# An S4 and gated-FFN training step on one core: the skip products of the last 16 row tiles made earlier and kept in DRAM

## The chip, the cores and the metric

The kernel runs on one core of one Trainium2 chip. The metric is the device time in microseconds (us) of one execution. A run executes the kernel several times; the time of the kernel before is the median of three. A profile is one execution recorded by the hardware profiler, and its times are that execution's own.

Engines are named as the profile names them: PE (TensorE, matmul), DVE (VectorE), ACT (ScalarE), POOL (GpSimd) and SP (SyncE, which here only issues DMA). Each runs its own instructions in order. A DMA that is issued by SP stands in SP's queue until the buffer that it writes is free and the data that it reads is there.

## The reference

A forward pass and all its gradients. With x of 2048 rows and D = 576 columns, and F = 4608:

```
xn  = layernorm(x)
out = x + (S4(xn) + xn * Dskip) + FFN(xn)
S4(xn)  = causal convolution of xn with a kernel K made from A, B, C, log_dt  (by FFT)
FFN(xn) = (relu(xn Wg) * (xn Wu)) Wd
```

The outputs are `out` (out_0), and for a given grad_out g the gradients of x (out_1), of the S4 parameters, of Dskip and of the three FFN weights. The gradient with respect to xn has the term g * Dskip from the same skip path; the gradient of x follows from it through the layernorm. So there are two skip terms: xn * Dskip in out_0, g * Dskip in the gradient.

## The kernel before

**Rows and chunks.** The 2048 rows are 16 row tiles t of 128, in four groups sg of four. F is cut into 12 chunks c of 384 columns. For each chunk, `a_unit` computes one third (ft) of a group's hidden gradients (three groups of five 512-wide matmuls, then L254 to L264 on VectorE); `outdx` multiplies them back to D columns for one row tile, in four quarters: output and gradient, each in two halves of 288 columns. `dw_down`, `dw_gu` and `dw_left` make the weight gradients of the chunk before. Within a chunk, `gen` yields two `outdx` after each of the first two `a_unit` of a group; the four `outdx` of the last group run one after the other at the start of the next chunk.

**Accumulating.** In chunks 0 to 10 the four quarters of a row tile are copied from PSUM to an SBUF tile `osx` of the pool `ffn_o`, which has three buffers, and added to `acc_dram` in DRAM by a DMA that GpSimd issues (L311 for chunk 0, L313 for the rest). An `osx` buffer is free again when that DMA has landed. PSUM has three banks for the FFN (`ps_mm`), three for S4 (`ps_s4`) and two for transposes (`pt`).

**S4.** The S4 part is a generator that runs beside the FFN, paced against it by the estimated microseconds that both yield. Its intermediate data goes through DRAM. It ends in chunk 11.

**The last chunk.** In chunk 11 `outdx` calls `Final` instead of copying. `Final.load(t)` fetches, on SP's queue and in this order, S3, two halves of Ct, xt, xn and g (the tile `f_xg`), and the accumulated row (`f_acc`), and makes both skip terms at once, L1030: `f_base` = `f_xg` * Dskip, 1152 elements a partition, bf16 in and F32 out. All of them are in a pool of three buffers. `begin(t)` loads up to tile t + 2. `terms` puts S4's last step, x and the accumulated row into the same PSUM group as the FFN's matmuls. `take` (L1049) adds a quarter of PSUM to `f_base`: the output's halves go to `f_o` and out to DRAM, the gradient's halves are written back into `f_base` as F32. `end` (L1058 to L1067) sends the gradient through the layernorm with `f_xg` (row sums on ACT and DVE, L1060 and L1061; L1064 to L1066) and stores it. `f_xg` of a tile is read last by L1066, so the loads of the tile three ahead into the same buffer wait for it.

**Order.** A scheduler of the language orders each engine's instructions from the program's order and its own estimates, so an edit can move other instructions too. `Balance` decides for each PSUM copy whether VectorE or ScalarE does it (L62, L68), from a running account of what both were given.

Of the kernel before, what the change touches and what calls it, by code (L numbers as in the profile page):

```python
# [9 lines left out]
BF16 = mybir.dt.bfloat16  # L10
F32 = mybir.dt.float32
# [3 lines left out]
P = 128  # L15
# [23 lines left out]
class Balance:  # L39


    def __init__(self, nc):
        self.nc = nc
        self.d = 0.0
        self.a = 0.0
# [115 lines left out]
class Ffn:  # L161
    def __init__(self, g, ctx, Wd_in, Wf_in, dWg, dWu, dWd):
        self.g = g
        self.Wd_in, self.Wf_in, self.dWg, self.dWu, self.dWd = Wd_in, Wf_in, dWg, dWu, dWd
        tc, nc = g.tc, g.nc
        pool = lambda name, bufs: ctx.enter_context(tc.tile_pool(name=name, bufs=bufs))
        wp = pool("ffn_w", 1)
        self.wd = [wp.tile([P, NK, Fc], BF16, name=f"wd{i}") for i in range(3)]
        self.wf = wp.tile([P, 3, FTC, D], BF16, name="wf")
        self.hN = wp.tile([P, ST, Fc], BF16, name="hN")  # L170
        self.dgN = wp.tile([P, ST, Fc], BF16, name="dgN")
        self.duN = wp.tile([P, ST, Fc], BF16, name="duN")
        g.xtp = pool("ffn_xt", 2)
        self.tp = pool("ffn_t", 2 * FTC - 1)
        self.ep = pool("ffn_e", 2)
        self.op = pool("ffn_o", 3)
        self.rp = pool("ffn_r", 2)
        self.dp = pool("ffn_d", 4)
        self.T = {}
        self.X = {}  # L180
        self.R = {}
        self.dh0 = {}

    def load_wd(self, c, which=(2, 0, 1)):

# [91 lines left out]
    def outdx(self, c, sg, j, last=None, turns=()):  # L277

        g, nc = self.g, self.g.nc
        t = sg * JS + j  # L280
        js = slice(j * P, (j + 1) * P)
        if last is None:
            o = self.op.tile([P, 2, D], BF16, name="osx")
        else:
            last.begin(t)
        src = self.t_steps(turns)
        Ts = [self.T[(c, sg, ft)] for ft in range(FTC)]
        for which in range(2):
            for hf in range(2):
                hs = slice(hf * DH, (hf + 1) * DH)  # L290
                if which == 0:
                    mms = [(Ts[ft][0], self.wf[:, 0, ft, hs]) for ft in range(FTC)]
                else:
                    mms = [(Ts[ft][1], self.wf[:, 1, ft, hs]) for ft in range(FTC)] + [(Ts[ft][2], self.wf[:, 2, ft, hs]) for ft in range(FTC)]
                mms = [(lt[:, js], rh) for lt, rh in mms]
                if last is not None:
                    mms = last.terms(t, which, hf) + mms
                ps = g.psum_mm.tile([P, 512], F32, name="ps_mm")
                for i, (lt, rh) in enumerate(mms):
                    nc.tensor.matmul(ps[:, :DH], lhsT=lt, rhs=rh, start=(i == 0), stop=(i == len(mms) - 1))  # L300
                if last is None:
                    g.bal.copy(o[:, which, hs], ps[:, :DH], DH)
                else:
                    last.take(t, which, hs, ps[:, :DH])
                next(src, None)
            if which == 0:
                yield FTC * 0.245
        if last is not None:
            last.end(t)
        elif c == 0:  # L310
            nc.gpsimd.dma_start(g.acc_dram[:, t, :, :], o[:])  # L311
        else:
            nc.gpsimd.dma_start(g.acc_dram[:, t, :, :], o[:], accum_op=ALU.add)  # L313
        yield FTC * 0.49
# [158 lines left out]
        return self.q.pop(i)  # L473

class S4:
    def __init__(self, g, par_in, log_dt, outs, Dskip):
        self.g, self.par_in, self.log_dt, self.outs, self.Dskip = g, par_in, log_dt, outs, Dskip
        dram = g.dram
        d = lambda name, shape, dt=BF16: dram.tile(shape, dt, name=name)
        self.s1_dram, self.s3_dram = d("s1_dram", [P, ST, 2, P]), d("s3_dram", [P, ST, 2, P])  # L480
        two = lambda name, shape: [d(f"{name}{hf}", shape) for hf in range(2)]
        self.A = {1: two("A_k", [P, ST, 1, 2, DH]), 2: two("A_ug", [P, ST, 2, 2, DH])}
        self.S = two("S_ug", [ST, P, 2, 2, DH])
        self.C = {1: two("C_dk", [P, ST, 1, 2, DH]), 2: two("C_ydu", [P, ST, 2, 2, DH])}
        self.dk_dram = two("dk_dram", [P, 4, DH // SC, 4, SC])
        self.k_dram = two("k_dram", [P, 4, DH // SC, 4, SC])
        self.dt_dram = d("dt_dram", [P, D], F32)
        self.ex_dram = d("ex_dram", [P, D // SX, SX, NE], F32)

    def pool(self, ctx, name, bufs, side="left"):  # L490
        return ctx.enter_context(self.g.tc.tile_pool(name=name, bufs=bufs, side=side, reuse_waits="tile"))
# [510 lines left out]
class Final:  # L1002

    def __init__(self, g, s4, Dskip, ctx):
        self.g, self.s4, self.Dskip, self.ctx = g, s4, Dskip, ctx
        self.parts = {}

    def load(self, t):  # L1010
        g, nc = self.g, self.g.nc
        if t == 0:
            pool = lambda name, bufs: self.ctx.enter_context(g.tc.tile_pool(name=name, bufs=bufs, reuse_waits="tile"))
            self.dsk = pool("fin1", 1).tile([P, D], BF16, name="dsk")
            nc.sync.dma_start(self.dsk[:], self.Dskip.rearrange("(o d) -> o d", o=1).to_broadcast([P, D]))
            self.pool = pool("fin3", 3)
        S3 = self.pool.tile([P, 2, P], BF16, name="S3")
        nc.sync.dma_start(S3[:], self.s4.s3_dram[:, t])
        Ct = self.pool.tile([P, 2, 2, 2, DH], BF16, name="bC2")
        for hf in range(2):  # L1020
            nc.sync.dma_start(Ct[:, hf], self.s4.C[2][hf][:, t])
        xt = self.pool.tile([P, D], BF16, name="xt")
        nc.sync.dma_start(xt[:], g.x_v[:, t, :])
        xg = self.pool.tile([P, 2, D], BF16, name="f_xg")
        nc.sync.dma_start(xg[:, 0, :], g.xn_dram[:, t, :])
        nc.sync.dma_start(xg[:, 1, :], g.g_v[:, t, :])
        acc = self.pool.tile([P, 2, D], BF16, name="f_acc")
        nc.sync.dma_start(acc[:], g.acc_dram[:, t])
        base = self.pool.tile([P, 2, D], F32, name="f_base")
        nc.vector.tensor_tensor(base[:], xg[:], self.dsk[:].unsqueeze(1).to_broadcast([P, 2, D]), op=ALU.mult)  # L1030
        g.bal.add(d=1.2)
        return S3, Ct, xt, xg, acc, base

    def begin(self, t):
        for n in range(t, min(t + 3, ST)):
            if n not in self.parts:
                self.parts[n] = self.load(n)
        self.o = self.pool.tile([P, 2, D], BF16, name="f_o")

    def terms(self, t, i, hf):  # L1040
        S3, Ct, xt, xg, acc, base = self.parts[t]
# [3 lines left out]

    def take(self, t, i, cols, ps):
        base = self.parts[t][5]
        dst = self.o[:, 0, cols] if i == 0 else base[:, 1, cols]
        self.g.nc.vector.tensor_tensor(dst, base[:, i, cols], ps, op=ALU.add)  # L1049
        self.g.bal.add(d=0.37)  # L1050

    def end(self, t):
        g, nc = self.g, self.g.nc
        S3, Ct, xt, xg, acc, base = self.parts[t]
        o = self.o
        inv_d = 1.0 / D
        xn, gt, dx = xg[:, 0, :], xg[:, 1, :], base[:, 1, :]
        nc.sync.dma_start(g.out0_v[:, t, :], o[:, 0, :])  # L1058
        m = self.pool.tile([P, 4], F32, name="f_m")
        nc.scalar.activation(acc[:, 1, :], dx, ACT.Copy, accum_out=m[:, 0:1])  # L1060
        nc.vector.scalar_tensor_tensor(acc[:, 0, :], dx, 1.0, xn, op0=ALU.mult, op1=ALU.mult, accum_out=m[:, 1:2])  # L1061
        nc.vector.tensor_scalar(m[:, 2:3], m[:, 1:2], -inv_d, None, op0=ALU.mult)
        nc.vector.tensor_scalar(m[:, 3:4], m[:, 0:1], -inv_d, g.rinv[:, t:t + 1], op0=ALU.mult, op1=ALU.mult)
        nc.vector.scalar_tensor_tensor(dx, xn, m[:, 2:3], dx, op0=ALU.mult, op1=ALU.add)  # L1064
        nc.scalar.activation(dx, dx, ACT.Identity, scale=g.rinv[:, t:t + 1], bias=m[:, 3:4])
        nc.vector.tensor_tensor(o[:, 1, :], dx, gt, op=ALU.add)  # L1066
        nc.sync.dma_start(g.out1_v[:, t, :], o[:, 1, :])  # L1067
        g.bal.add(d=2.5, a=1.1)

@with_exitstack  # L1070
def kernel(
# [44 lines left out]

    outs = dict(A_re=out_2, A_im=out_3, B_re=out_4, B_im=out_5, C_re=out_6, C_im=out_7, log_dt=out_8)
    ffn = Ffn(g, ctx, Wd_in, Wf_in, out_10, out_11, out_12)
    s4 = S4(g, par_in, A_log_dt, outs, A_Dskip)
    lnctx, fctx = ExitStack(), ExitStack()  # L1120
    ln_pools = [lnctx.enter_context(tc.tile_pool(name=n, bufs=4)) for n in ("ln_sb", "ln_small")]
    ffn.ln_sb = ln_pools[0]
# [6 lines left out]
            lnctx.close()  # L1129
        return r  # L1130

    final = Final(g, s4, A_Dskip, fctx)
    sgen = s4.gen()
    ft = stt = 0.0
    start = None
# [71 lines left out]
```

## Time and profile before

| what | us |
|---|---|
| median of the three runs (lowest, highest) | 1861.03 (1860.21, 1864.52) |
| the profiled execution, its own time | 1864.52 |
| its span in the trace | 1862.4 |
| PE busy | 1753.3 |
| VectorE busy | 1327.2 |
| ScalarE busy | 1164.1 |
| L1030, all 16: busy, and idle time of VectorE just before it | 21.7, 21.0 |
| `acc_dram` DMAs: median time from issue to landing | 5.0 |
| `f_xg` DMAs (two of 144 KB a tile): the same | 3.9, 4.0 |
| `f_acc` DMAs (288 KB a tile): the same | 4.3 |

The first `outdx` of the last kind starts at 1710.9 us and the last one ends at 1822.5 us. Chunks two to nine lie between about 330 and 1540 us. The mean granted clock of TensorE is 0.991.

How to read what the prediction shows. A window line has the stretch, its length, the busy time of each engine with its number of instructions, the clock granted to TensorE as a share of the full one, the mean busy share of the 16 DMA engines and the rate. A line of waits has the waiting engine, line and tile, what ended the wait, the sum in us, how many and the longest. A group's line has line, engine, operation and shapes, then busy time and the mean of one in ns, then the engine's idle time just before. A timeline line has start and length in us, and in brackets how long the engine stood idle before, and what ended that. L numbers are lines of the kernel before.

### The profile page before, as it was taken

To read this page: it belongs to the slowest core of one execution; us is meant where nothing else is said; L and a number is where in the kernel's file an instruction comes from. 1 tells how busy PE (TensorE), PEld (TensorE's weight loads), DVE (VectorE), ACT (ScalarE), POOL (GpSimd) and SP (SyncE) were. 2 spreads that over 40 slices of the span, in tenths; PEclk is the share of its full clock that TensorE was granted. 3 is DMA by queue.
4 is the path that set the end of the run, shared out by engine and by line. 5 is a ranking of instruction groups with operands and counts; after the bars stand their busy time and mean duration, and the time that the engine had idled before them with its cause. 6 is when DMAs were issued, how large, how long until landed. Compare 5 with 4: busy or idle time off the path is not lost.

```text
span 1862.4 us, 42002 instructions
## 1 busy us (share of the span) xinstructions
PE 1753.3 (94%) x16449; PEld 1222.3 (66%) x16449; DVE 1327.2 (71%) x3041; ACT 1164.1 (63%) x2618; POOL 204.7 (11%) x244
## 2 busy tenths in 40 slices
PE   7989999999999999999989999999999998989889
PEld 5665667667667667666656766766766865666666
DVE  7565784677786886786688789688788774743872
ACT  5864863786586587477378568558658745742442
POOL 0200112011012012011102011101102101100000
PEclk9999999999999999999999999999999999999999
DMA  8889989677568558568667756766846858876863
GB/s 293 272 293 324 321 213 267 189 192 226 165 150 226 170 116 208 167 152 222 193 161 173 222 139 148 225 162 140 220 152 114 206 158 241 236 221 185 247 206 102
DMA packets 215929, 373.25 MB, mean 200 GB/s; under 512 B 49202, under 2 KB 128564, under 8 KB 214196
## 3 DMA queue, kind: packets, MB, share of 16 engines
q1 hardware_dynamic: 189764, 304.08, 50.2%
q0 software_dynamic: 24384, 51.92, 18.6%
q10 hardware_dynamic: 1584, 14.60, 2.2%
q8 instruction: 128, 2.10, 0.5%
q14 instruction: 69, 0.57, 0.1%
HBM read 233.08 MB, written 137.43 MB: 199 GB/s over the span
## 4 chain that ended last, share of the span: by engine, by line
PE 52%; DVE 22%; DMA 12%; ACT 8%; issue 5%; SPq 1%; POOL 1%; ACTq 0%; DVEq 0%; POOLq 0%
PE ps_mm L244 13%; PE ps_mm L300 12%; PE ps_mm L354 10%; PE ps_mm L338 6%; DMA acc_dram<-osx 3%; PE pt L273 2%; DVE pr L902 2%; DVE Sm L903 2%; DVE Y L849 2%; DMA f_xg<-in_grad_out_dram 2%; DVE V L848 1%; DVE Y L847 1%; DVE upm L254 1%; DMA ex_dram<-exs 1%; PE ps_mm L372 1%
## 5 line engine op out<-in xcount | busy, mean ns | idle before, releaser
L68 ACT CAST osx<-ps_mm 128x288 bf16<-128x288 f32 x675 | 258.0, 423 | 78.6 <-PE ps_mm L300 63.9
L313 POOL DMA_DIRECT2D acc_dram<-osx x160 | 138.2, 864 | 1061.0 <-ACT osx L68 594.7
L300 PE MATMUL ps_mm<-wf,dgT 128*128 128x288 bf16 x1152 | 205.6, 287 | 16.6 <-ACT osx L68 9.8
L354 PEld LDWEIGHTS <-rows 128*128 128x128 bf16 x1536 | 146.6, 98 | 92.4 <-issue 2.4
L300 PE MATMUL ps_mm<-wf,duT 128*128 128x288 bf16 x1152 | 206.1, 287 | 0.0
L300 PE MATMUL ps_mm<-wf,hT 128*128 128x288 bf16 x1152 | 184.3, 288 | 6.0 <-DVE hT L256 3.5
L244 PE MATMUL ps_mm<-xT,wd_158 128*128 128x512 bf16 x720 | 180.1, 379 | 4.0 <-DVE osx L62 1.9
L244 PE MATMUL ps_mm<-gT,wd_160 128*128 128x512 bf16 x705 | 179.3, 384 | 4.2 <-ACT obw L68 3.9
L244 PE MATMUL ps_mm<-xT,wd_159 128*128 128x512 bf16 x720 | 180.0, 379 | 0.0
L254 DVE SCALAR_TENSOR_TENSOR upm<-rg,ps_mm 128x512 bf16<-128x512 bf16 x144 | 98.3, 683 | 92.8 <-PE ps_mm L244 64.7
L338 PE MATMUL ps_mm<-rows,hN 128*128 128x144 bf16 x2304 | 161.1, 228 | 0.0
L338 PEld LDWEIGHTS <-hN 128*128 128x128 bf16 x2304 | 150.7, 99 | 7.4 <-issue 4.1
L300 PEld LDWEIGHTS <-dgT 128*128 128x128 bf16 x1152 | 110.2, 98 | 54.0 <-issue 27.5
L68 ACT CAST obw<-ps_mm 128x384 bf16<-128x384 f32 x104 | 49.6, 477 | 146.3 <-PE ps_mm L354 95.5
L354 PE MATMUL ps_mm<-duN,rows 128*128 128x384 bf16 x768 | 136.8, 326 | 0.4 <-DVE upm L254 0.4
L354 PE MATMUL ps_mm<-dgN,rows 128*128 128x384 bf16 x768 | 136.4, 326 | 0.6 <-ACT rg L252 0.6
L300 PEld LDWEIGHTS <-duT 128*128 128x128 bf16 x1152 | 112.7, 98 | 29.1 <-issue 0.5
L300 PEld LDWEIGHTS <-hT 128*128 128x128 bf16 x1152 | 108.0, 98 | 34.3 <-DVE hT L256 5.4
L68 ACT CAST dhb<-ps_mm 128x512 bf16<-128x512 f32 x141 | 83.4, 592 | 65.4 <-PE ps_mm L244 63.9
L252 ACT ACTIVATE rg<-ps_mm 128x512 bf16<-128x512 f32 x144 | 86.8, 603 | 58.7 <-PE ps_mm L244 56.1
L903 DVE TENSOR_REDUCE Sm<-pr 128x8 f32<-128x256 f32 x288 | 119.5, 415 | 4.0
L244 PEld LDWEIGHTS <-wd_160 128*128 128x128 bf16 x705 | 64.7, 98 | 67.9 <-issue 12.9
(2881 smaller groups left out, 3601.5 us busy)
## 6 DMA issues: line engine op xcount, KB each, us to landing
acc_dram<-osx POOLq DMA_DIRECT2D x176, 288.0 KB, 5.0
gT<-in_gT_dram SPq DMA_DIRECT2D x48, 640.0 KB, 6.1
xT<-xT_dram SPq DMA_DIRECT2D x44, 640.0 KB, 5.9
rows<-in_gq_dram SPq DMA_DIRECT2D x48, 576.0 KB, 4.5
wf<-in_Wf_dram ACTq DMA_DIRECT2D x11, 1296.0 KB, 8.9
ex_dram<-exs SPq DMA_DIRECT2D x18, 640.0 KB, 6.2
ex<-ex_dram SPq DMA_DIRECT2D x36, 320.0 KB, 3.7
out_dram<-obw SPq DMA_DIRECT2D x96, 96.0 KB, 2.7
```

The costliest lines, as they stand in the source:

```text
L68: self.nc.scalar.copy(out, in_)
L244: nc.tensor.matmul(ps[:], lhsT=w[:, k, fs], rhs=rhs[:, k, :], start=(k == 0), stop=(k == NK - 1))
L252: nc.scalar.activation(rg[:], ps_g[:], ACT.Relu)
L254: nc.vector.scalar_tensor_tensor(upm[:], rg[:], 0.0, ps_u[:], op0=ALU.is_gt, op1=ALU.mult)
L273: nc.tensor.transpose(out=pt[:, j, :], in_=src[:, j * P:(j + 1) * P], identity=g.ident_bf[:])
L300: nc.tensor.matmul(ps[:, :DH], lhsT=lt, rhs=rh, start=(i == 0), stop=(i == len(mms) - 1))
L313: nc.gpsimd.dma_start(g.acc_dram[:, t, :, :], o[:], accum_op=ALU.add)
L338: nc.tensor.matmul(ps[:, ft * 144:(ft + 1) * 144], lhsT=self.hN[:, st, ft * P:(ft + 1) * P], rhs=gq[:, st, :], start=(st == 0), stop=(st = ...
L354: nc.tensor.matmul(ps[:, :Fc], lhsT=xs[:, st, 0:P], rhs=src[:, st, :], start=(st == 0), stop=(st == ST - 1))
L849: v.tensor_tensor(Y[:], Y[:], V[:], op=ALU.add)
L902: nc.vector.tensor_tensor(pr[:], X[:, dx:dx + DG, r0:r0 + 2].rearrange("p d r a -> p d (r a)").unsqueeze(2).to_broadcast(sh), psg[:, 0:DG ...
L903: nc.vector.tensor_reduce(out=Sm[:, vi, s0 + dd:s0 + dd + DG, :], in_=pr[:], op=ALU.add, axis=AX.X)
```

## The change

The products xn * Dskip and g * Dskip are made in chunks two to nine instead of in the last chunk. In chunk c, `outdx` of the row tiles t with t mod 8 = c - 2 (two a chunk, 16 in all) takes one more `osx` buffer and loads xn and g of that tile into it, on SP's queue. The next `outdx` multiplies that buffer by Dskip in place, all bf16, and SP stores it to a new DRAM tensor `base_dram`. In the last chunk `f_base` is loaded from there, as bf16, behind the other loads of the tile; the gradient's halves go to an F32 tile `f_dx` of their own. Dskip is loaded once at the start, by GpSimd, and stays in SBUF.

```diff
@@ Ffn.outdx, after the four quarters
+        if self.skip is not None:
+            sk, n = self.skip
+            nc.vector.tensor_tensor(sk[:], sk[:], g.dsk[:].unsqueeze(1).to_broadcast([P, 2, D]), op=ALU.mult)
+            g.bal.add(d=0.8)
+            nc.sync.dma_start(g.base_dram[:, n], sk[:])
+            self.skip = None
+        if t % 8 == c - 2:
+            sk = self.op.tile([P, 2, D], BF16, name="osx")
+            nc.sync.dma_start(sk[:, 0, :], g.xn_dram[:, t, :])
+            nc.sync.dma_start(sk[:, 1, :], g.g_v[:, t, :])
+            self.skip = sk, t
         if last is not None:
             last.end(t)
@@ Final.load
-            self.dsk = pool("fin1", 1).tile([P, D], BF16, name="dsk")
-            nc.sync.dma_start(self.dsk[:], self.Dskip.rearrange("(o d) -> o d", o=1).to_broadcast([P, D]))
...
-        base = self.pool.tile([P, 2, D], F32, name="f_base")
-        nc.vector.tensor_tensor(base[:], xg[:], self.dsk[:].unsqueeze(1).to_broadcast([P, 2, D]), op=ALU.mult)
-        g.bal.add(d=1.2)
+        base = self.pool.tile([P, 2, D], BF16, name="f_base")
+        nc.sync.dma_start(base[:], g.base_dram[:, t])
@@ Final.begin
+        self.dx = self.pool.tile([P, D], F32, name="f_dx")
@@ Final.take
-        dst = self.o[:, 0, cols] if i == 0 else base[:, 1, cols]
+        dst = self.o[:, 0, cols] if i == 0 else self.dx[:, cols]
@@ Final.end
-        xn, gt, dx = xg[:, 0, :], xg[:, 1, :], base[:, 1, :]
+        xn, gt, dx = xg[:, 0, :], xg[:, 1, :], self.dx[:]
@@ the kernel's body
+    g.base_dram = d("base_dram", [P, ST, 2, D])
+    g.dsk = g.consts.tile([P, D], BF16, name="dsk")
+    nc.gpsimd.dma_start(g.dsk[:], A_Dskip.rearrange("(o d) -> o d", o=1).to_broadcast([P, D]))
```

The rest of the diff takes Dskip out of the arguments of `S4` and `Final`.

More of the change, by code (lines that the diff above doesn't have):

```diff
@@ L307, in outdx @@
                 yield FTC * 0.245
+        if self.skip is not None:
[3 more added lines that the diff above has]
+            nc.sync.dma_start(g.base_dram[:, n], sk[:])
+            self.skip = None
+        if t % 8 == c - 2:
[3 more added lines that the diff above has]
+            self.skip = sk, t
         if last is not None:
@@ L475, with __init__ @@
 class S4:
-    def __init__(self, g, par_in, log_dt, outs, Dskip):
-        self.g, self.par_in, self.log_dt, self.outs, self.Dskip = g, par_in, log_dt, outs, Dskip
+    def __init__(self, g, par_in, log_dt, outs):
+        self.g, self.par_in, self.log_dt, self.outs = g, par_in, log_dt, outs
         dram = g.dram
@@ L1002, with __init__ @@
 class Final:
-    def __init__(self, g, s4, Dskip, ctx):
-        self.g, self.s4, self.Dskip, self.ctx = g, s4, Dskip, ctx
+    def __init__(self, g, s4, ctx):
+        self.g, self.s4, self.ctx = g, s4, ctx
         self.parts = {}
@@ L1118 @@
     ffn = Ffn(g, ctx, Wd_in, Wf_in, out_10, out_11, out_12)
-    s4 = S4(g, par_in, A_log_dt, outs, A_Dskip)
+    g.base_dram = d("base_dram", [P, ST, 2, D])
+    g.dsk = g.consts.tile([P, D], BF16, name="dsk")
+    nc.gpsimd.dma_start(g.dsk[:], A_Dskip.rearrange("(o d) -> o d", o=1).to_broadcast([P, D]))
+    s4 = S4(g, par_in, A_log_dt, outs)
     lnctx, fctx = ExitStack(), ExitStack()
@@ L1130, in ln @@
         return r
-    final = Final(g, s4, A_Dskip, fctx)
+    final = Final(g, s4, fctx)
     sgen = s4.gen()
```

## The prediction

> **What bounds the kernel now.** I read the page's busy shares and chain first, then busy time by stretch, then the waits of the one stretch that the change aims at, then the stretches it adds work to.
>
> ```profile
> PE 1753.3 (94%) x16449; PEld 1222.3 (66%) x16449; DVE 1327.2 (71%) x3041; ACT 1164.1 (63%) x2618; POOL 204.7 (11%) x244
> ...
> PE 52%; DVE 22%; DMA 12%; ACT 8%; issue 5%; SPq 1%; POOL 1%; ACTq 0%; DVEq 0%; POOLq 0%
> ```
>
> TensorE is 94% busy, so at most 109 us can be won anywhere, and only where PE stands still. Most of the span it does not: from 330 to 1530 us it is busy 1162 of 1200 us. The stage in which the 16 final row tiles are finished (1711 to 1822.5 us) is different:
>
> ```profile
> core 0: us, PE busy (x) PEld busy (x) DVE busy (x) ACT busy (x) POOL busy (x), PEclk, DMA share, GB/s
> 1711.00:1822.50 111.50, 100.39 (x758) 69.89 (x756) 91.07 (x200) 47.55 (x93) 0.00 (x0) 0.97 0.70 214
> ...
> 1725.00:1740.00 15.00, 13.08 (x100) 8.34 (x97) 12.34 (x27) 8.16 (x16) 0.00 (x0) 1.00 0.83 260
> 1755.00:1770.00 15.00, 13.78 (x106) 9.42 (x105) 13.12 (x28) 7.13 (x15) 0.00 (x0) 1.00 0.83 247
> 1785.00:1800.00 15.00, 14.05 (x108) 9.63 (x107) 13.47 (x32) 7.33 (x15) 0.00 (x0) 1.00 0.83 251
> ```
>
> ```profile
> DVE f_base L1030 <- DMA f_xg<-in_grad_out_dram: 11.4, 9, 2.2
> ...
> PE pt L273 <- DVE dgT L262: 6.3, 3, 2.6
> PE ps_mm L300 <- DVE f_o L1049: 4.5, 4, 1.9
> ...
> L1030 DVE TENSOR_TENSOR f_base<-f_xg,dsk 128x1152 f32<-128x1152 bf16 x13 | 17.6, 1357 | 11.6 <-DMA f_xg<-in_grad_out_dram 11.4
> ```
>
> VectorE works 91.1 us here and stands 11.4 us more in front of its multiply L1030, waiting for a tile that was requested only after an earlier tile gave up its buffer. Together that is 102.5 of 111.5 us: VectorE sets the pace, and every PE wait in the stage (6.3, 4.5 and 0.2 us) names it. What PE alone would need, by its timeline: a final tile is 32 matmuls, 3.92 us (1710.93 to 1714.85), 16 times 62.7; eight a_units of three 1.08 us groups, 25.9; 122 transposes at 0.056 us, 6.8. Sum 95.4, so 16.1 us of the stage are lost to waits, and to the lower clock (0.97) that the windows show with them. What follows the stage (39.5 us of weight gradients) waits for none of it but its end, so what is won here is won at the end.
>
> The first three final tiles are loaded much earlier, and the same multiply blocks VectorE there:
>
> ```profile
> 1548.32 1.36 DVE L1030 TENSOR_TENSOR f_base<-f_xg,dsk 128x1152 f32<-128x1152 bf16 x1 [2.79 <-DMA f_xg<-xn_dram]
> 1551.23 1.36 DVE L1030 TENSOR_TENSOR f_base<-f_xg,dsk 128x1152 f32<-128x1152 bf16 x1 [1.55 <-DMA f_xg<-in_grad_out_dram]
> ...
> 1558.27 1.36 DVE L1030 TENSOR_TENSOR f_base<-f_xg,dsk 128x1152 f32<-128x1152 bf16 x1 [5.09 <-DMA f_xg<-in_grad_out_dram]
> ...
> 1558.42 0.40 PE L608 MATMUL ps_s_25937<-kk,Sx 128*128 128x288 bf16 x1 [4.69 <-ACT fA_25907 L68]
> ```
>
> **The change, part by part.** Durations are those of the profiled execution: 1864.5 us, of which 1862.4 are its span. It is 3.5 us above the median of the runs, 1861.0; I add the differences to the median.
>
> (1) *Final stage.* Gone from VectorE: 13 x 1.357 = 17.6 us of work and 11.4 us of waits. What comes: a base load of 288 KB a tile on SP's queue, the last of each tile's loads, and L1049 (the take) now waits for it. The take's own length I leave at 0.45 us (L62, a PSUM-to-bf16 copy of the same size, has 0.455); dx has a tile of its own, still F32. VectorE falls to 91.1 - 17.6 = 73.5 us and no longer sets the pace; next is PE with 95.4. Then the DMA engines. They work 0.70 x 111.5 = 78 us here. Full, they move about 300 GB/s in this part of the program (306 at share 1.03 from 1590 to 1600 us), and 13 x 0.295 MB = 3.8 MB more takes 12.8 us: 91 us, close to PE's 95. In the three stretches above, two base loads in 15 us add 39 GB/s, 0.13 of a share: 0.83 becomes 0.96 at the old pace. So 45 of the 111 us can speed up by hardly 2 us; the other 66 can.
> By the Trainium skill, page "DMA: Bandwidth & Descriptors", Specifications, the limit per core is about 358 GB/s of HBM; by that rule the 27.7 MB of the stage (214 GB/s in 111.5 us, and 3.8 MB) would take an estimated 77 us, DMA would never bind, and this term would be the full 16 us. The rows at share 1.0 contradict it, at 265 to 311 GB/s.
>
> The base load is also late by construction: in the built order of the changed kernel it stands behind the next tile's xg loads, which wait for the end of the tile three back. Its like, f_acc, takes 3.5 to 6.5 us to land. After that end about 7 to 8 us remain to the take (one more tile, one a_unit, the first quarter, less the 4.5 us in which the end's chain runs), of which issue takes 1 to 3. So some takes will wait 1 to 2 us; three PSUM banks of quarters (0.86 us each) cover most of that. Bounds: -16 (PE alone) and -2 (DMA full, or base late every time). I take half of the 16: -8.
>
> (2) *The early burst, 1540 to 1560 us.* VectorE loses 9.4 us of waits and 4.1 us of work. The same stretch has DMA shares of 1.01 and 1.06, and gets 0.88 MB more, 2.9 us. The PE stall of 4.69 us hangs on an A_k store that took 7.4 us to land behind these loads. In the built order part of the third tile's loads moves behind several A_k stores. Bounds -5 (stall gone, and a little) and +3 (burst longer by its bytes); I take -2.
>
> (3) *What is added in chunks two to nine.* Sixteen times: two loads of 144 KB, a multiply, a store of 288 KB, in a third osx buffer.
> The multiply is all bf16. The nearest rows are L634 (128x576, 0.454 us) and L849 (128x1024, 0.701); 1152 wide gives 0.78, 16 times 12.5 us. VectorE idles about 270 of the 1200 us there, and its Y tiles are ready 4.8 us or more (median 23) before PE takes them, so the work itself is nearly covered: 0 to 3 us. If that cover were gone it would cost the 12.5.
> The new wait is the multiply's for its load. Behind it in VectorE's queue stand upm (L254), which frees a PSUM bank that PE needs within a group or two, and pr (L902), which frees one of S4's three. I placed each multiply between its neighbours in the trace of before, and its load after SP's preceding issue plus 4 to 4.5 us. Eight arrive in time, or into an idle gap of VectorE. Eight are late, by 0.5 to 5 us (near 815, 1330 and 1480 us most), 18 us together. Only part reaches PE: 2 us, between 0 and 8.
> SP gets 48 issues of 0.45 us. Its store waits for the multiply, and xT, gT and rows loads stand behind it; by the same placement SP was idle there in before except for 1 to 2 us three times, and those loads run a block or more ahead: nothing.
> The buffer costs most. With three osx tiles an outdx writes into the one freed two tiles ago; with a skip tile in between, the one freed one tile ago. The acc stores land after a median of 5.1 us and up to 10.4, and the wait already shows:
>
> ```profile
> ACT osx L68 <- DMA acc_dram<-osx: 11.5, 9, 2.4
> ...
> 1183.36 0.53 PE L300 MATMUL ps_mm<-wf,dgT 128*128 128x288 bf16 x3 [1.08 <-ACT osx L68]
> ```
>
> Taking evacuation starts and landings of before, one buffer less costs ScalarE about 4 us at 1179 us, 3 at 1031, 1 to 2 at 1330 and up to 2 at 878; elsewhere the store has landed 1 us or more before it is needed. Some 9 us, and PE, in its own order behind three banks, gives back half: 4 us, between 0 and 9.
> Dskip's early load on GpSimd's queue and 63 more SP issues overlap everything. Part (3): 1 + 2 + 4 = +7, bounds 0 and +18 (the last term's 9, 8 and 1 to 3 of work).
>
> **Sum.** -8 - 2 + 7 = -3: 1858.0 us at the median, about 1861.5 as a profiled execution.
>
> **Rivals.**
> *B, cover everywhere.* Base loads land in time, the final stage runs at PE's pace (-13), the burst loses its stall (-4), the added work hides in VectorE's 270 idle us (+2): -15, 1846. For it: every PE wait in the final stage names VectorE. Against: DMA at 0.96 in three stretches.
> *C, the stolen buffer decides (slower).* Place: the osx tile taken by a skip row in the runs of four consecutive outdx at chunk starts, where tiles follow in 2.2 to 3 us and stores land in 5 to 10. ScalarE, then PE, stop for a whole landing. From about 1 us of PE time for each of the 16 skips (+16) it outweighs a final gain of 6: +10, 1871. For it: 1.08 us of PE stall at 1183 already. Against: in twelve of the 16 places the stores have landed.
> *D, DMA is the new bound at the end.* Base arrives late for most tiles, the final stage wins 2, the burst grows by 2, the middle costs 6: +6, 1867. For it: 0.83 of share before 288 KB more a tile. Against: the stage's mean is 0.70.
>
> **How the numbers follow.** About 0.3% (5.6 us) is what a measurement of this kernel can tell from no change: under 1855.4 is faster, over 1866.6 slower. My forecast has 0.45 and a range of its own of 1850 to 1864; a quarter of it (0.11) lies under 1855.4. B 0.20, all faster. C 0.22, all slower. D 0.13, half slower. Faster 0.31, same 0.40, slower 0.29. The range runs from B's centre to just past C's, 1846 to 1872, and leaves out a tenth on each side.
>
> **What would show it.** Right: no L1030 in the final window, VectorE near 74 us there, the window near 103, DMA share near 0.9, takes waiting for f_base a few times by 1 to 2 us; from 330 to 1530 us PE's idle time grows from 38 to about 45, with ScalarE's wait for acc_dram growing from 11.5 us. Wrong in (1): window under 99 (B) or over 108 with f_base waits in PE's or VectorE's list (D). Wrong in (3): idle time in the middle unchanged, or grown by over 12 us with osx named. Wrong as a whole: a changed time in a stage that has neither a skip tile nor a final tile, which would be the reordering of instructions and none of these costs.

## The result: 1.1% slower, and the profile after

| | before | after |
|---|---|---|
| median of the runs compared (us) | 1860.6 (1856.6 to 1864.5) | 1880.1 (1877.9 to 1886.2) |
| after / before, 95% interval | | 1.011 (1.0077 to 1.0143) |
| the profiled execution, and its span | 1864.5, 1862.4 | 1886.2, 1883.4 |

The forecast was 1858.0 with a range of 1846 to 1872. The change did in the final stage more than was forecast, and cost in chunks two to nine twice its upper bound.

From here on, L numbers are lines of the changed kernel (in an experiment, of that run's own kernel), one above those of before just ahead of the skip block and ten to twelve above behind it. The skip multiply is L311, its loads L317 and L318, its store L313. The page's first and chain lines, to set against those of before:

```profile
PE 1764.0 (94%) x16449; PEld 1229.5 (65%) x16449; DVE 1317.3 (70%) x3038; ACT 1167.1 (62%) x2621; POOL 204.7 (11%) x245
...
PE 54%; DVE 20%; DMA 11%; ACT 8%; issue 5%; POOL 1%; SPq 0%; ACTq 0%; DVEq 0%; POOLq 0%
```

PE has the same 16449 matmuls and is busy 10.7 us longer, with a mean granted clock of 0.984 in place of 0.991. The page does not say where. For that I took the start of every a_unit's hT product (L256 before, L257 after) as a milestone and subtracted the two profiles:

| at the first a_unit of chunk | 2 | 4 | 5 | 6 | 7 | 8 | 9 | 10 | 11 | last a_unit |
|---|---|---|---|---|---|---|---|---|---|---|
| after minus before, us | 1.5 | 4.3 | 5.1 | 13.3 | 21.4 | 25.3 | 27.8 | 35.7 | 36.4 | 26.1 |

So 34.2 us are lost between chunks 2 and 10, 0.7 in chunk 10 (the early burst), and 15.4 us are won behind chunk 11's start (36.4 down to 21.0 at the end of the span). Within a chunk the loss is not spread: 24 of the 34.2 us fall into five short pieces at the starts of chunks 6 to 10 (3.9, 6.6, 2.8, 2.7 and 7.9 us), where the four `outdx` of the last group run one after the other; 3.0 and 2.8 more are two single skip tiles, at 512 and 819 us.

The final stage, first by window (stretch, length, busy time of PE, PEld, DVE, ACT, POOL, clock, DMA share, GB/s), then two lines of its list of waits:

```profile
1748.00:1844.00 96.00, 95.85 (x758) 68.56 (x757) 75.95 (x187) 47.77 (x92) 0.00 (x0) 1.00 0.89 289
```

```profile
ACT f_acc L1070 <- DVE f_dx L1059: 32.1, 15, 3.8
...
DVE f_dx L1059 <- PE ps_mm L301: 9.5, 14, 0.9
```

The stage takes 96.0 in place of 111.5 us, PE is busy all of it at full clock, and VectorE now waits for PE. No engine waits for `f_base`; PE waits for nothing.

The stretch 330 to 1530 us, by its waits (sum, times, longest):

```profile
DVE osx L311 <- DMA osx<-in_grad_out_dram: 35.6, 10, 9.2
...
ACT osx L68 <- DMA acc_dram<-osx: 18.3, 7, 4.9
...
PE ps_mm L301 <- ACT osx L68: 15.2, 20, 4.3
...
PE ps_s_24952 L896 <- DVE pr L914: 5.6, 1, 5.6
```

VectorE stands 35.6 us in front of the new multiply. ScalarE's wait for an accumulating store to land has grown from 11.1 (in this stretch) to 18.3 us, PE's wait for ScalarE's `osx` copies from 8.9 to 15.2, and a wait of 5.6 us for VectorE's `pr` is new.

Two places show the two ways. First t 12, at the start of chunk 7, on three engines:

```profile
1045.33 0.90 PE L301 MATMUL ps_mm<-wf,hT 128*128 128x288 bf16 x6
...
1047.94 0.76 DVE L311 TENSOR_TENSOR osx<-osx,dsk 128x1152 bf16<-128x1152 bf16 x1 [3.30 <-DMA osx<-in_grad_out_dram]
...
1050.80 1.00 ACT L68 CAST osx<-ps_mm 128x288 bf16<-128x288 f32 x3 [4.88 <-DMA acc_dram<-osx]
1051.25 0.88 PE L301 MATMUL ps_mm<-wf,dgT 128*128 128x288 bf16 x3 [4.29 <-ACT osx L68]
...
1052.64 1.64 PE L301 MATMUL ps_mm<-wf,hT 128*128 128x288 bf16 x6
```

ScalarE has no `osx` buffer to copy into, because one of the three holds a skip tile, and stands 4.88 us until a store lands; PE follows for 4.29 us. And when PE resumes, six matmuls that took 0.90 us take 1.64. The clock shows it:

```profile
882.76:886.16 3.40, 3.18 (x18) 2.31 (x19) 0.83 (x3) 2.44 (x6) 0.00 (x0) 0.50 0.96 366
1050.01:1056.82 6.81, 5.57 (x24) 3.43 (x24) 0.03 (x1) 2.60 (x7) 0.85 (x1) 0.50 0.44 85
1205.20:1212.00 6.80, 6.38 (x84) 5.51 (x84) 6.39 (x13) 4.24 (x12) 1.71 (x2) 1.00 0.75 136
1517.64:1524.45 6.81, 4.97 (x43) 4.97 (x43) 6.78 (x16) 1.51 (x4) 0.00 (x0) 0.50 0.74 230
```

The granted clock drops to 0.50 some 3 to 4 us into the stall of 4.3 us here and into one of 5.6 us at 1514, and stays there for 6.8 us, of which PE works 5.6 and 5.0. After a stall of 2.5 us at 880 it is 0.50 for 3.4 us; after one of 3.4 us at 1202 it stays at 1.00. The Trainium skill, page "TensorE: Matmul & The Clock Gate", Part 1 ("What's actually happening"), says: idle for one activity window of about 3.4 us, the array runs at half its clock until a busy window has passed. The 3.4 us, and twice that, agree with such a window; half speed after a stall of 2.5 us and none after 3.4 us is not what the rule in this form would give.

The second place is t 15, at the start of chunk 10, by the chain of waits (start, length, what):

```profile
1506.98 9.15 DMA osx<-in_grad_out_dram
...
1516.35 0.76 DVE osx L311
1517.11 0.60 DVE V L860
1517.71 0.34 DVE pr L914
...
1519.48 1.01 PE ps_s_24952 L896 x8
```

A 144 KB load takes 9.15 us to land, and VectorE waits for it with everything behind: `V` and `pr`, which frees the S4 bank that PE waits for.

Why so late? The DMA issues around t 12 (KB each, us from issue to landing):

```profile
xT<-xT_dram SPq DMA_DIRECT2D x1, 640.0 KB, 8.9
gT<-in_gT_dram SPq DMA_DIRECT2D x1, 640.0 KB, 10.0
...
wd_159<-in_Wd_dram SPq DMA_DIRECT2D x1, 480.0 KB, 7.7
...
osx<-in_grad_out_dram SPq DMA_DIRECT2D x1, 144.0 KB, 7.7
```

At a chunk's start the skip rows share the DMA engines with the next chunk's weights and transposed inputs, and land with them.

The bill for 330 to 1530 us, in windows of 2 us: PE's idle time grew from 38.1 to 60.7 us, and PE's busy time times (1 - granted clock) from 1.5 to 13.0. Together 34.1 us, which is the 34.2 of the milestones. A third of the loss is clock.

### The profile page after: what moved, and what is told of

Read it like the earlier page. It is cut to its first block, busy times and chain, and to the rows that moved or that the text cites. A ratio compares the mean times of both kernels' runs of the same rounds, so it can differ in the third digit from the quotient of the medians.

```text
span 1883.4 us, 42137 instructions
## 1 busy us (share of the span) xinstructions
PE 1764.0 (94%) x16449; PEld 1229.5 (65%) x16449; DVE 1317.3 (70%) x3038; ACT 1167.1 (62%) x2621; POOL 204.7 (11%) x245
## 3 DMA queue, kind: packets, MB, share of 16 engines
q0 software_dynamic: 24432, 52.06, 18.3%
## 4 chain that ended last, share of the span: by engine, by line
PE 54%; DVE 20%; DMA 11%; ACT 8%; issue 5%; POOL 1%; SPq 0%; ACTq 0%; DVEq 0%; POOLq 0%
PE ps_mm L245 14%; PE ps_mm L301 13%; PE ps_mm L366 10%; PE ps_mm L350 6%; PE pt L274 2%; DVE pr L914 2%; DMA acc_dram<-osx 2%; DVE Sm L915 2%; DVE Y L861 2%; DVE V L860 1%; DVE Y L859 1%; ACT osx L68 1%; DVE upm L255 1%; DMA osx<-in_grad_out_dram 1%; PE ps_mm L384 1%
```

## The experiments

Two theories. **W**: VectorE's in-order wait for the skip load. **B**: the stolen `osx` buffer. (**R**, that only the order of instructions changed, stood beside them.) Each run below has its median, its ratio to the kernel before with the 95% interval, the growth of the middle by the milestones (chunk 2 to chunk 10, one profile), and from 330 to 1530 us the wait at the multiply and ScalarE's wait for the landing of `acc_dram`, all in us.

| run | median | ratio | middle | at multiply | ScalarE |
|---|---|---|---|---|---|
| changed kernel | 1880.1 | 1.011 (1.0077 to 1.0143) | +34 | 35.6 | 18.3 |
| e1 final alone | 1851.0 | 0.993 (0.990 to 0.996) | +2 | none | 11.0 |
| e2 middle alone | 1898.0 | 1.018 (1.016 to 1.020) | +32 | 34.2 | 19.1 |
| e3 early places | 1857.1 | 0.997 (0.994 to 0.999) | +7 | 7.1 | 11.5 |
| e4 rows buffer, lag three | 1846.7 | 0.991 (0.988 to 0.993) | -2 | 4.7 | 9.8 |
| e5 two behind | 1877.8 | 1.008 (1.006 to 1.010) | +31 | 33.4 | 19.8 |
| e6 wait without osx | 1860.7 | 0.998 (0.996 to 0.999) | +4 | 5.8 | 10.7 |
| e7 rows, lag one | 1850.3 | 0.993 (0.990 to 0.995) | +5 | 5.5 | 13.9 |
| e8 rows, GpSimd | 1865.5 | 1.001 (1.000 to 1.003) | +15 | 0 on VectorE | 9.9 |
| e9 held two | 1872.8 | 1.005 (1.002 to 1.007) | +20 | 12.6, not for the load | 21.8 |
| e10 held one | 1863.3 | 1.001 (0.999 to 1.003) | +17 | 5.9, 0.8 of it for the load | 23.1 |
| e11 load only | 1859.7 | 0.998 (0.996 to 0.999) | +8 | none | 12.5 |
| e12 base twice | 1849.2 | 0.992 (0.989 to 0.995) | +1 | 4.8 | 10.7 |

One profile carries several us of chance: e4 and e7 have the same order of instructions on PE and VectorE, and their middles differ by 7, their medians by 3.6. The profiles of e10 and e11 are the fastest of their ten runs, 3.8 and 4.7 us under their medians.

**e1, the final stage alone**

```diff
-        if t % 8 == c - 2:
+        if False:
...
-        nc.sync.dma_start(base[:], g.base_dram[:, t])
+        nc.sync.dma_start(base[:], g.acc_dram[:, t])
```

> Final stage alone: no skip tile is loaded, multiplied or stored in the middle chunks, and the final stage loads into f_base 295 KB of acc_dram in place of base_dram, so the same DMA and DVE work there (the skip terms are left out of the two outputs). Theory M (the final stage gives 15.5 us, the middle stage costs all the rest): about 1861 - 15 = 1846 us, idle of TensorE at 330 to 1530 us back near 38 us. Theory S (the prediction's sum: the final stage is worth 8 us): about 1853. Theory R (the order of the instructions was changed by the extra yields and DRAM tiles, not by the skip work): 1860 or more.

12 us less than the kernel before (1863.1, measured beside it), midway between what M and S forecast. The stage itself is as M has it: it takes 96.5 us at full clock, and by the milestones 15.3 us are won behind chunk 11's start, not the sum's 8. The profile loses 1.8 us ahead of chunk 2, which no skip tile can have caused. The early load of Dskip is the likely cause: at the first a_unit of all, the twelve runs that have it are 1.7 to 3.4 us behind the kernel before, and e6, the one without it, 0.2.

**e2, the middle alone**: `Final` as in the kernel before.

```diff
-        base = self.pool.tile([P, 2, D], BF16, name="f_base")
-        nc.sync.dma_start(base[:], g.base_dram[:, t])
+        base = self.pool.tile([P, 2, D], F32, name="f_base")
+        nc.vector.tensor_tensor(base[:], xg[:], g.dsk[:].unsqueeze(1).to_broadcast([P, 2, D]), op=ALU.mult)
```

> Middle stage alone: the skip tiles are loaded, multiplied and stored as in the changed kernel, and the final stage multiplies f_base itself as in the kernel before (what is stored is not read). Theory M: 1880 + 15.5 = about 1895 us, that is 35 us for sixteen tiles that take 12 us on VectorE. Theory S (middle +7): about 1868. If the two halves disturb each other, the sum of this and of the final stage alone differs from +19 by more than 5.

+35 us. With e1's -12 that is +23, where the whole change has +19.5: the halves add up.

**e3, other places**

```diff
-        if t % 8 == c - 2:
+        if 2 <= c <= 9 and t in (1, 6):
+            n = c - 2 + (8 if t == 6 else 0)
```

> The changed kernel with the same sixteen loads, still in the osx pool and multiplied one outdx later, but always after outdx 1 and 6 of a chunk, so that none falls in the run of four outdx at the start of the next chunk. Theory B (the stolen buffer costs in the runs of four, where four outputs come in a row): the steps of t 12 to 15, together about 20 us of the 36, go: about 1860 us. Theory W (the in-order wait of VectorE for the load costs wherever it is): stays within 5 us of 1880. Theory R: any time, with VectorE's waits at the multiply short.

23 us less than the changed kernel, with as many skip tiles in the same pool. Its waits from 330 to 1530 us:

```profile
ACT osx L68 <- DMA acc_dram<-osx: 11.5, 7, 2.4
...
PE ps_mm L301 <- ACT osx L68: 9.9, 22, 2.5
...
DVE osx L311 <- DMA osx<-in_grad_out_dram: 7.1, 5, 3.7
```

ScalarE's and PE's waits are back near the values of before. R falls: the order of the instructions was changed here too. B and W both lose their ground away from the runs of four, so the place decides, but not which of the two.

**e4, no `osx` buffer and a long lag**

```diff
-        if self.skip is not None:
+        if self.skip is not None and t == self.skip[2] + 3:
...
-            sk = self.op.tile([P, 2, D], BF16, name="osx")
+            sk = self.dp.tile([P, ST, 144], BF16, name="rows")[:].rearrange("p t d -> p (t d)")[:, 0:2 * D].rearrange("p (i d) -> p i d", d=D)
```

with places t 0 and 3.

> The changed kernel with the skip tile in a buffer of the rows pool, which holds nothing in the first half of a chunk, so no osx buffer is taken; loads after outdx 0 and 3, multiplied three outdx later instead of one. Takes away both suspects, buffer and wait. Theories B and W alike: the sixteen multiplies of 0.76 us are left, half of them beside idle time: 1846 to 1852 us, VectorE's waits for the skip loads under 3 us in sum. Theory R or traffic (27 MB less slack for the accumulating stores, reordering): 1865 or more.

Faster than both kernels: 16.4 us under the one before. The multiply's group in 330 to 1530 us (busy, mean ns of one, idle time of VectorE before it):

```profile
L311 DVE TENSOR_TENSOR rows<-rows,dsk 128x1152 bf16<-128x1152 bf16 x16 | 12.0, 752 | 4.7 <-DMA rows<-in_grad_out_dram 2.7 <-DMA A_ug<-fA 1.9
```

Sixteen multiplies of 0.75 us, and no time lost to e1, which has none: that part of the sum (0 to 3 us) was right.

**e5, a longer lag as the code has it**

```diff
-        if self.skip is not None:
+        if self.skip is not None and (t - self.skip[1]) % ST == 2:
```

> The changed kernel with places and osx buffer as they are, and the multiply issued two outdx after its load instead of one. VectorE's wait for the load shrinks, the osx buffer is held longer: its store is issued at the end of outdx t+2, just before outdx t+3 needs that buffer. Theory W (VectorE's in-order wait for the load): 1880 - 15 = 1865 us or less, with the waits at the multiply from 35.6 to under 10 us. Theory B (the stolen osx buffer): no gain or slower, 1880 to 1895, with the wait of ScalarE's osx copies for the landing of a store up from 18 us.

Inconclusive on the lag: the scheduler put the sixteen multiplies at the same places of VectorE's order as in the changed kernel, up to six instructions. It serves as a second measurement of that kernel.

**e6, the wait alone**

```diff
-            nc.vector.tensor_tensor(sk[:], sk[:], g.dsk[:].unsqueeze(1).to_broadcast([P, 2, D]), op=ALU.mult)
+            nc.vector.tensor_tensor(sk[:], sk[:], sk[:], op=ALU.mult)
...
-            sk = self.op.tile([P, 2, D], BF16, name="osx")
+            sk = self.kp.tile([P, D], BF16, name="skp")
```

> Same places and lag as in the changed kernel, but the skip tile is half the size in a buffer of its own, so no osx buffer is taken; the room for it comes from leaving out the D_skip tile, the multiply is tile by itself over 576 columns (0.4 in place of 0.76 us), only the grad row is loaded and stored, and the final stage loads acc_dram in place of base_dram (the skip terms are left out). Only the in-order wait of VectorE for a load is left. Theory W: waits at the multiply of 25 us or more, time 1868 to 1880. Theory B: the waits may be there, but the time is 1846 to 1855 as without skip work.

The places are not the same: with a buffer of its own nothing holds the loads back, and all sixteen multiplies stand between 71 and 378 us, six of them before 150 us. The 5.8 us of the table count from 330 us on; over the whole run VectorE waits 20.1 us for these loads:

```profile
DVE skp L312 <- DMA skp<-in_grad_out_dram: 20.1, 10, 7.7
```

No `osx` buffer is taken, and the median is 9.7 us over e1's. By the milestones this run falls 13 us behind e1, all of it between the first skip tile and the last, and stays level from there to chunk 6. So the wait alone costs, and about half of it or a little more reaches the end, though these are other places than the changed kernel's.

**e7, rows buffer, other places and lag one**

```diff
-        if 2 <= c <= 9 and t in (0, 3):
+        if 2 <= c <= 9 and t in (1, 6):
...
-        if self.skip is not None and t == self.skip[2] + 3:
+        if self.skip is not None and t == self.skip[2] + 1:
```

> The rows buffer again, but the places of the run with early places (after outdx 1 and 6) and the multiply one outdx behind its load: against that run (1857) only the buffer differs, against the run with the rows buffer and lag three (1847) the places and the lag. Theory B: the osx buffer was what cost the 10 us between those two: 1847. Theory W: the short waits at the multiply (7 us there) and the lag were: about 1857.

The scheduler made the same order here as in e4, loads included (the first at 325.7 and 326.5 us): a repetition of e4. Place and lag in the code decide only as far as a buffer holds the load back. Against e3 the buffer, and the earlier loads that it allows, are worth 7 to 10 us.

**e8, the multiply on GpSimd**

```diff
-            nc.vector.tensor_tensor(sk, sk, g.dsk[:].unsqueeze(1).to_broadcast([P, 2, D]), op=ALU.mult)
+            nc.gpsimd.tensor_tensor(sk, sk, g.dsk[:].unsqueeze(1).to_broadcast([P, 2, D]), op=ALU.mult)
...
-            nc.sync.dma_start(g.base_dram[:, n], sk)
+            nc.gpsimd.dma_start(g.base_dram[:, n], sk)
```

> The rows buffer, loads after outdx 0 and 3, lag three, with the multiply and the store moved to GpSimd, which is busy for a tenth of the span: VectorE loses its sixteen multiplies (12 us). If those cost what part of them VectorE does not do beside other work, 2 to 6 us less than 1847; if they were hidden, the same; if GpSimd's multiply holds up the accumulating stores that are issued on the same engine, or slows VectorE, 1850 or more.

19 us slower than e4. VectorE is rid of 12 us of work, but while GpSimd multiplies it is held up:

```profile
929.37 0.42 DVE L257 TENSOR_TENSOR hT<-rg,upm 128x512 bf16<-128x512 bf16 x1
929.70 2.58 DVE L263 TENSOR_TENSOR dgT<-dhb,upm 128x512 bf16<-128x512 bf16 x1
```

```profile
929.54 2.46 POOL L311 TENSOR_TENSOR rows<-rows,dsk 128x1152 bf16<-128x1152 bf16 x1 [9.46 <-DMA rows<-in_grad_out_dram]
```

dgT takes 2.58 us, where hT, of the same size, takes 0.42. Fourteen of the sixteen multiplies stretch one VectorE instruction so, 22 us in all, more than VectorE was spared. GpSimd itself was idle for 154 us in front of these multiplies until their loads had landed, with accumulating stores behind; but ScalarE's wait for such stores did not grow (9.9). So the hold-up of VectorE is the likelier cause of the 19 us; the two were not separated.

**e9 and e10, a lag that the scheduler can't undo**

```diff
-            nc.vector.tensor_tensor(sk[:], sk[:], g.dsk[:].unsqueeze(1).to_broadcast([P, 2, D]), op=ALU.mult)
+            nc.vector.tensor_tensor(sk[:], sk[:], o[:], op=ALU.mult)
```

and in e9 the condition of e5 as well.

> The order of the run with the multiply two outdx behind turned out to be that of the changed kernel, since the scheduler moved the multiply back up. Here it can't: the multiply's second operand is the osx tile of the outdx two behind (instead of D_skip, so the skip terms come out scaled by other numbers), and the load, the osx buffer and the places stay. By the built order t15's and t14's multiply move down by 100 instructions of VectorE, most others by 5 to 20, and the buffer is held longer. Theory W: waits at the multiply for the load fall under 15 us and the time to 1850 to 1868, in proportion (about 1 us of time for each us of wait). Theory B: ScalarE's wait for acc_dram landings rises over 18 us and the time stays at 1875 or more.

> The same with the osx tile of the next outdx as second operand: the multiply can't stand ahead of where the diff writes it. t15's moves down by 100 instructions, those of t12 to t14 by 2 or 3 only. Theory W: only t15's wait of 9 us and some short ones go: 20 to 27 us of waits and 1866 to 1874. Theory B: as the changed kernel, 1876 to 1884, since the buffer is held as long.

e10 separates the theories best. The wait for the load is gone (0.8 us in all, where 20 to 27 were expected to stay), and the time falls by 17 us. VectorE waits 5.1 us for copies of the `osx` tile instead. What is left is mostly B; here again t 12, ScalarE and PE:

```profile
1037.76 1.00 ACT L68 CAST osx<-ps_mm 128x288 bf16<-128x288 f32 x3 [3.72 <-DMA acc_dram<-osx]
1038.21 0.75 PE L301 MATMUL ps_mm<-wf,dgT 128*128 128x288 bf16 x3 [3.13 <-ACT osx L68]
```

Its middle grows in the same pieces at the starts of chunks 6 to 9 (+5.4, +4.4, +3.4, +3.0), and no longer at chunk 10's (-0.1), where the changed kernel lost 7.9 us: t 15's loss was all wait. The piece at chunk 6 is another loss than the changed kernel's, though. There the changed kernel stands beside a late load, and ScalarE waits for no store; PE waits for the `hT` behind the multiply:

```profile
881.11 0.76 DVE L311 TENSOR_TENSOR osx<-osx,dsk 128x1152 bf16<-128x1152 bf16 x1 [4.92 <-DMA osx<-in_grad_out_dram]
...
882.98 0.42 PE L301 MATMUL ps_mm<-wf,hT 128*128 128x288 bf16 x1 [2.46 <-DVE hT L257]
```

In e10, which holds the buffer longer, ScalarE waits 6.5 us for a store at that place and PE 5.6. So e10 pays a buffer loss that the changed kernel did not have, and its 17 us are more likely too little for the wait than too much.

e9 lies between its two forecasts: no wait for the load either, but 12.6 us of VectorE waiting for the copies of the `osx` tile that it now reads, and the buffer held longest, with 21.8 us on ScalarE. A long lag in a stolen buffer pays one cost with the other.

**e11, the buffer alone**

```diff
-            nc.vector.tensor_tensor(sk[:], sk[:], g.dsk[:].unsqueeze(1).to_broadcast([P, 2, D]), op=ALU.mult)
             g.bal.add(d=0.8)
-            nc.sync.dma_start(g.base_dram[:, n], sk[:])
```

> Places, osx buffer and loads as in the changed kernel, no multiply and no store, and the final stage loads acc_dram for base_dram (the skip terms are left out); the account that balances copies is booked as if the multiply were there. The buffer is taken until the load has landed, VectorE waits for nothing new. Theory W: 1848 to 1856, as the final stage alone (1851). Theory B: 1865 or more, with ScalarE's wait for acc_dram landings at 15 us or more.

Between the forecasts: 9 us over e1, with the buffer taken only until its load has landed. But ScalarE's wait, 12.5 us, stays under the 15 that B gave as its sign.

So both theories are right, and neither alone. Over e1 (1851.0) the changed kernel is 29 us longer. Taking the wait for the load away (e10) gives back 17 us; the other 12 go with the buffer, 9 of them already while the load is under way (e11). The changed kernel's own pieces say much the same, sorted by what stood still at each: 17.6 us at a late load (512 and 819 us, chunks 6 and 10), 12.1 us at a missing buffer (chunks 7 to 9), 4.5 us in smaller pieces. Either split is good to a few us. No run loads at the same places without taking an `osx` buffer. But the two stores ahead of each stall land in the changed kernel about as before at chunks 8 and 9 (after 6.2 to 7.5 us, before 6.3 to 7.6) and 1.6 to 1.7 us later only at chunk 7, so the loads' own traffic is a small part of the 12. The multiplies themselves are worth nothing that shows (e4).

**e12, is DMA near its limit at the end?**

```diff
         nc.sync.dma_start(base[:], g.base_dram[:, t])
+        again = self.pool.tile([P, 2, D], BF16, name="f_again")
+        nc.sync.dma_start(again[:], g.base_dram[:, t])
```

> The kernel with the rows buffer (1847) and one more load of 288 KB a tile in the final stage, the same base row into a tile that nobody reads: 4.7 MB more in a stage that moved about 28 MB in 96 us (289 GB/s at a share of 0.89). By the rows at share 1.0 (265 to 311 GB/s) this is past full, 4.7 MB / 300 = 16 us less 11 us of room left: 1850 to 1860, with waits for f_base. By the skill's 358 GB/s, 49 GB/s more is still under the limit: 1847.

```profile
1708.00:1808.00 100.00, 97.88 (x757) 69.25 (x756) 76.71 (x188) 47.73 (x92) 0.00 (x0) 0.98 0.94 318
```

```profile
PE ps_mm L301 <- DMA f_acc<-acc_dram: 1.9, 1, 1.9
...
DVE f_o L1062 <- DMA f_base<-base_dram: 1.7, 1, 1.7
```

4.7 MB more are moved in 4 us more of stage, at 318 GB/s and a share of 0.94, and two waits for loads appear that no profile with one load a tile has. The median, 1849.2, is 2.4 us over e4's, within the intervals, and lies between the two forecasts. So the rows at share 1.0, 265 to 311 GB/s, were no ceiling, since 318 were moved; but with twice the base loads DMA begins to show.

## Why the prediction was wrong, step by step

**(1) Final stage: right mechanism, term too small.** VectorE was the bound and PE's 95.4 us the floor; the stage took 96.0. The term was -8 and measured -15.4, close to its bound of -16. What halved it was the fear of DMA: a ceiling of 300 GB/s read from stretches with share 1.0, and a base load late by construction. No take waited for `f_base` (loads landed after 3.8 to 7.6 us), the stage ran at 289 GB/s, and e12 moves 318. A share of 1.0 at 265 to 311 GB/s was no ceiling: the changed kernel moves 382 GB/s at a share of 1.04 from 1040 to 1046 us. The rule weighed against it, the 358 GB/s of the Trainium skill's page "DMA: Bandwidth & Descriptors" (Specifications), gave the right verdict on this stage, though the 382 GB/s of the other stretch go beyond its figure.

**(2) Early burst: -2 forecast, +0.7 measured.** Its multiplies and their waits are gone, but PE's stall there stayed (4.15 after 4.69 us, for the same `fA` copy): VectorE was not what held it. In e4 and e11 this piece gained 5 us; why there and not here was not tried.

**(3) Middle: +7 forecast, bounds 0 and +18, +34 measured. This is the step that failed.** The two causes were named, and so was the sign of being wrong (idle time grown by over 12 us, with `osx` named; it grew by 22.6). What failed is what each costs TensorE.
- *The wait for the load.* 18 us on VectorE were forecast, 2 of them reaching PE. 35.6 us came, about 17 reaching the end. The eight late ones were sized by landing 4 to 4.5 us after issue, which holds in the middle of a chunk (2.1 to 5.2 us in the changed kernel); at the chunks' starts four of five took 5.4 to 9.2 us, among the weights. And the share that reaches PE was taken as a ninth, though the text itself named what stands behind: `upm` and `pr`, each the release of a PSUM bank. About half is what it was.
- *The buffer.* ScalarE's side was about right: 9 us more wait forecast, 7.2 measured, at three of the four places (1031, 1179 and 1330 us forecast; 1051, 1205 and 1357 measured, later by what was lost until then). The fourth, 878 us, came true as a number only: the loss at 880 is a late load. Wrong was that PE, behind three banks, "gives back half": 4 us forecast, 12 measured. PE waited there for ScalarE nearly as long as ScalarE for the store (4.3 of 4.9 us, 3.4 of 3.4, 3.6 of 3.8), and the clock came on top.
- *The clock* was in no term. 11.5 of the 34 us are work done at a lower granted clock after the stalls; they are part of the two costs above, not beside them. The profile of before showed it (0.97 in the final stage), and the prediction noted it there without pricing it for stalls to come.

The work term, 1 us, was right. Dskip's early load, said to overlap everything, seems to cost some 2 us at the start (see e1); no run tries it alone.

**The rivals.** C had the direction, the place and one of the two mechanisms, but laid all of it on the buffer and, with a final gain of only 6, reached 1871. B's final stage (-13) came closest. D fell with the changed kernel itself, where no take waits for `f_base`. The true case was B's end with more than C's middle, a combination that no rival held.

## What to carry to other kernels

An instruction that waits for a small load holds up everything behind it in its engine's order, and for the load's landing at that place, not its median landing: look at what else is issued just ahead of it, and move it to where that queue is quiet. When a scratch buffer is needed, count the tiles in flight at the busiest place, and take one from a pool that is empty at that time; the same sixteen products cost 29 us at busy places in a pool in use, and nothing at quiet places in one at rest. Price a stall of TensorE with its clock: here 22.6 us of added idle time came with 11.5 us lost to a lower clock.

## What was not expected of the hardware

- The granted clock of TensorE was 0.50 for 6.8 us from within stalls of 4.3 and 5.6 us on, for 3.4 us after one of 2.5 us, and not at all after one of 3.4 us.
- A GpSimd multiply of 128x1152 bf16 (2.4 us) held VectorE's product of two SBUF tiles for its whole length (2.58 in place of 0.42 us), while `pr`, which reads PSUM, kept its 0.42 us beside it. The Trainium skill, page "SBUF — State Buffer", section "SBUF: two separate sides", states the same: the two engines share a pair of ports under an exclusive lock, and the loser stands still.
- Loads of 144 KB took from 2.1 to 9.2 us to land; the longest were issued at chunks' starts, among loads of 480 and 640 KB.
